# AFNO on Trainium2: the second chunk's remainder rows copied block by block, and the scratch read of the other chunks' rows issued one slot behind their writes

## The chip, the cores and the metric

The kernel runs on one core of one Trainium2 chip. The metric is device time in microseconds (us) of one execution. The kernel before takes 1431.06 us, the median of three timed runs (1430.18, 1431.06 and 1435.22 us). One further execution was profiled.

The core's engines are named as the profile names them: PE (matmul; PEld is its weight load), ACT (ScalarE), DVE (VectorE), POOL (GpSimd) and SP, which here only issues DMAs. Each engine works through its own list of instructions in order and waits on semaphores of the others.

## The reference

Two blocks in a row: an AFNO block (a 2-D FFT over 4096 positions, per-block complex MLP on the frequencies, shrinkage, inverse FFT) and a SwiGLU feed-forward block, both behind an adaptive layer norm. The change lies in the AFNO block. Cut to it:

```python
def _A_ref(x, w1, b1, w2, b2):               # x: 1 x 1 x 4096 x 640, NB = 4 blocks of BS = 160 channels
    Xf = rfft2(x, axes=(1, 2))
    z = Xf.reshape(B, H, Wf, NB, BS)
    zr, zi = z.real, z.imag
    hr = einsum('bhwni,nio->bhwno', zr, w1[0]) - einsum('bhwni,nio->bhwno', zi, w1[1]) + b1[0]
    hi = einsum('bhwni,nio->bhwno', zi, w1[0]) + einsum('bhwni,nio->bhwno', zr, w1[1]) + b1[1]
    hr, hi = relu(hr), relu(hi)
    or_ = einsum(hr, w2[0]) - einsum(hi, w2[1]) + b2[0]
    oi_ = einsum(hi, w2[0]) + einsum(hr, w2[1]) + b2[1]
    # soft shrinkage of both by 0.01, then irfft2
x = x + ga * _A_ref(layernorm(x) * (1 + ca) + sa, ...)
x = x + gb * _B_ref(layernorm(x) * (1 + cb) + sb, ...)      # silu(x @ w_gate) * (x @ w_up) @ w_down
```

## The kernel before

**Chunks and slots.** The frequencies are worked off in 8 chunks (0 to 7) of four blocks each. One pass of the loop at L833 is called a slot here: slot p handles chunk ch = p // 4 and block b = p % 4, for p = 0 to 28. In slot p the PE does the first MLP layer of block p (`stage_l1`, L652, matmuls L667 and L680), the second DFT stage of a block that comes later (`stage_b`, L593, matmul L599), the second MLP layer of block p - 1 (`stage_l2`, L701, matmul L717) and the inverse DFT of block p - 6 (`stage_i`, L753, matmul L763).

**The remainder rows.** A block has 160 channels, but a matmul takes 128 rows. So `stage_b` runs five times per chunk: t = 0 to 3 for the first 128 channels of each block, and t = 4 for the last 32 channels of all four blocks together. The fifth result must be regrouped: the first layer needs, for each block, a tile slice `rz[:, b]` of 128 partitions in which the 32 channels stand four times (real and imaginary part, each as a high and a low half in reduced float32). The kernel before has two ways to do that:

- **Chunk 0: block by block.** `evac_rh` (L633, ACT, two copies of 32x256 at L639) takes the high halves of one block straight from PSUM into `rz`, `evac_rl` (L642, DVE, two operations of 32x256 at L649) the low halves. The result of `stage_b(0, 4)` stays in its PSUM bank (tag `b1`) until the fourth block is copied. The list `rows` at L853 says which blocks are copied in which slot.
- **Chunks 1 to 7: through scratch memory.** `evac_b` (L602) takes the whole result with one ACT copy (L607) and one DVE operation (L608) of 128x512 into `z`; `move_r` (L619) then has SP issue four writes of 128 KB to a DRAM scratch `rzd` (L623) and one read of 512 KB back into `rz` (L625). The read waits for the writes.

**What sets the order.** The order of this part is written out by hand, one list per engine. SP's list around the change, for chunk ch + 1, is: in slot 4 ch (b = 0) the four moves of the chunk before (`move_x`, L736, `xx<-tt`, 320 KB each), in slot 4 ch + 1 the four writes and the read of `move_r`, in slot 4 ch + 3 the loads of the chunk after (`load_g`, L306, 1280 KB, and `load_tb`, L296, 256 KB). For chunk 1 the writes and the read stand in slot 2, and `load_g(2)` behind them. A dictionary `mods` adds in most slots a load of 320 KB of `w_mod` (`mod_load`, L534) at the end of the slot; a load waits for the DVE addition (`mod_add`, L539 and L541) that frees its buffer. SP stops at a read that waits, and all its later DMAs with it. Towards the end of the chunks `load_first_rows` (L828) reads back parts of the result.

The feed-forward block behind that (from L1399 on) is ordered by a planner at build time; the change does not touch it.

```python
        if q[1] < 4 or q[0]:                 # L848: all but the remainder rows of chunk 0
            evac_b(*q)
    ...
    rows = [p + 2] * (p < 2)                 # L853
    ...
    if todo and todo[0][1] == 4:             # L880: the slot of stage_b(ch + 1, 4)
        move_r(todo[0][0])
```

Of the kernel before, what the change touches and what calls it, by code (L numbers as in the profile page):

```python
# [21 lines left out]
NCH = 8  # L22
# [149 lines left out]
def body(tc, x, w1, b1, w2, b2, wg, wu, wd, c, wm, k_fa, k_tb, k_tx, k_bm, k_bx, k_ga, k_ge, k_id, out, dbg=None):  # L172
    nc = tc.nc
# [3 lines left out]
    def f32(ap):  # L177
        return ap.bitcast(F32)
# [21 lines left out]
    with ExitStack() as top:  # L200
# [35 lines left out]
        with ExitStack() as af:  # L236
# [40 lines left out]
            def weights_high(w, h, l, v, sg, eng=None):  # L277
                if eng:
                    eng.tensor_scalar(w[:, :, h], v, sg, None, op0=OP.mult)
                else:  # L280
                    act.activation(w[:, :, h], v, AF.Copy if isinstance(sg, float) else AF.Identity, scale=sg)

            def weights_low(w, h, l, v, sg):
                dve.scalar_tensor_tensor(w[:, :, l], v, sg, f32(w[:, :, h]), op0=OP.mult, op1=OP.subtract)
# [9 lines left out]
            def load_tb(ch):  # L294
                tb = lp.tile([P, 4, 128], F32, tag="tb", bufs=2, name=f"tb{ch}")
                nc.sync.dma_start(tb, k_tb[:, 4 * ch:4 * ch + 4])  # L296
                tbs[ch] = tb


            def load_g(ch, us=None):  # L300
                if ch not in gs:
                    gs[ch] = fx.tile([P, 4, D], F32, tag="gx", bufs=2, name=f"g{ch}")
                f, e = (ch, 1) if ch < 2 else (2, 2) if ch < 4 else (3, 4)
                src = s1[f].rearrange("(u v) (q e j) d -> e u (v q) (j d)", u=4, e=e, q=4)[ch % e]
                if us is None:
                    nc.sync.dma_start(gs[ch].rearrange("p j d -> p (j d)"), src.rearrange("u r d -> r u d"))  # L306
                else:
                    for u in us:
                        nc.sync.dma_start(gs[ch][u:P:4].rearrange("p j d -> p (j d)"), src[u])
# [276 lines left out]
            rzs = {}  # L586
            hss = {}
            rzd = [nc.dram_tensor(f"rzd{i}", (4, 32, NB, 258), F32, kind="Internal").ap() for i in range(2)]

            def width(ch):  # L590
                return 258 if ch == CE else 256

            def stage_b(ch, t, tag=None):  # L593
                g, tb = gs[ch], tbs[ch]
                pb = (ps.tile([P, 2, 256], F32, tag=tag, name=f"pb{ch}_{t}") if tag else
                      bank0(1 if t == 4 else 0, [P, 2, 256], f"pb{ch}_{t}"))
                col = slice(128 * t, 128 * t + 128)
                for j in range(4):
                    mm(pb[:, :, 64 * j:64 * j + 64], g[:, j, col], tb[:, j, :], start=True, stop=True)  # L599
                pbs[ch, t] = pb  # L600

            def evac_b(ch, t):  # L602
                pb = pbs[ch, t]
                z = (lp.tile([P, 2, 2, 258], F32R, tag="z", bufs=4, name=f"z{ch}_{t}") if t < 4 else
                     hp.tile([P, 2, 2, 258], F32R, tag="zr", bufs=1, name=f"z{ch}_{t}"))
                zs[ch, t] = z
                act.activation(z[:, 0, :, 0:256], pb, AF.Identity, scale=ca1[:, t:t + 1])  # L607
                dve.scalar_tensor_tensor(z[:, 1, :, 0:256], pb, ca1[:, t:t + 1],  # L608
                                         f32(z[:, 0, :, 0:256]), op0=OP.mult, op1=OP.subtract)
                if ch == CE:  # L610
                    pool.tensor_copy(z[:, 0, :, 0:257:256], f32(edge[:, 0, t]))
                    pool.tensor_copy(z[:, 1, :, 0:257:256], f32(edge[:, 1, t]))
                    pool.tensor_copy(z[:, :, :, 257], zero[:, 0, 0])


            def new_r(ch):
                rzs[ch] = hp.tile([P, NB, 258], F32R, tag="rz", bufs=2, name=f"rz{ch}")

            def move_r(ch):  # L619
                NN = width(ch)  # L620
                d = rzd[ch % 2]
                for q in range(4):
                    nc.sync.dma_start(d[q, :, :, :NN].rearrange("r b e -> b r e"), f32(zs[ch, 4][:, q // 2, q % 2, :NN]))  # L623
                new_r(ch)
                nc.sync.dma_start(f32(rzs[ch][:, :, :NN]), d[:, :, :, :NN].rearrange("q r b e -> (q r) b e"))  # L625

            def evac_r(ch, b, part=None):
                if part != 1:
# [104 lines left out]
            def move_x(ch, i):  # L733
                q, h = i // 2, i % 2
                xx = p2.tile([P, D], F32, tag="xx", bufs=5, name=f"xx{ch}_{i}")
                nc.sync.dma_start(xx, tts[ch, q][64 * h:64 * h + 64])  # L736
                xxs[ch, i] = xx
# [88 lines left out]
            def load_first_rows(lo, hi, q, e=slice(0, D)):  # L826
                for k in range(2):
                    q.dma_start(cf[k][lo:hi, :, e], s2[lo:hi, 2 * k:2 * k + 2, e])  # L828
# [4 lines left out]
            for p in range(LAST + 1):  # L833
                ch, b = p // 4, p % 4
                on(shrink, p - 6)
                on(stage_l1, p)


                if p < 4:
                    todo = ([(0, 2)], [(0, 3)], [(1, 4), (1, 0)], [(1, 1)])[p]  # L840
                elif b == 0:
                    todo = [(ch, 3)]
                else:
                    todo = [(ch + 1, 4)] * (b == 1) + [(ch + 1, b - 1)]
                todo = [q for q in todo if q[0] < NCH]
                for q in todo:
                    stage_b(*q)
                    if q[1] < 4 or q[0]:  # L848
                        evac_b(*q)
                for f, *a in sums.get(p, ()):  # L850
                    f(*a)

                rows = [p + 2] * (p < 2)  # L853
                for k in rows:
                    on(evac_rh, k)
                if p == 0:
                    weights_high(*prep2[4])
                on(tail_l1, p)
                if p == 0:
                    weights_low(*prep2[2])  # L860
                for k in rows:
                    on(evac_rl, k)
                if p == 3:
                    adds = []
                    stage_l2(0, 2, held=adds)
                    stage_b(1, 2)
                    evac_b(1, 2)
                    on(tail_low, p)
                    for f in adds:
                        f()  # L870
                else:
                    on(tail_low, p)
                    on(stage_l2, p - 1)
                on(stage_i, p - 6)
                if p < LAST:
                    on(shrink_parts, p - 5)
                if b == 0 and ch:
                    for i in range(4):
                        move_x(ch - 1, i)
                if todo and todo[0][1] == 4:  # L880
                    move_r(todo[0][0])
                if p == 0:
                    weights_low(*prep2[4])
                    pool.memset(zero, 0.0)
                    pool.tensor_copy(edge, zero)
                    nc.sync.dma_start(bm.rearrange("p a b -> p (a b)"), k_bm)
                if p == 2 or b == 3 and 2 < ch + 2 < NCH:
                    load_g(ch + 2)
                    load_tb(ch + 2)
                for f, *a in mods.get(p, ()):  # L890
                    f(*a)
                if p == LAST - 4:
                    cf += [rp.tile([P, 2, D], F32, tag=tag, name=f"cf{tag}") for tag in ("rm", "rr")]
                    load_first_rows(rb + 16, rl, nc.sync)
                elif p == LAST - 1:
                    load_first_rows(0, rb - 16, nc.sync)
# [154 lines left out]
        with ExitStack() as ff:  # L1051
# [161 lines left out]
            def chain(at=None):  # L1213
                c = Chain()
                chains.insert(len(chains) if at is None else at, c)
                return c
# [162 lines left out]
            rows = [[chain() for _ in range(4)] for _ in range(NT)]  # L1379
# [1058 lines left out]
            for t in range(NS):  # L2438
                for n in range(NW):
                    if sum_at(n) == t:  # L2440
                        a, b = sum_w(n)
# [81 lines left out]
```

## Time and profile before

| | |
|---|---|
| median of three timed runs | 1431.06 us |
| profiled execution, its own time | 1424.83 us |
| its span (first to last instruction) | 1423.0 us |
| PE / DVE / ACT / POOL busy in the span | 1384.5 / 1025.1 / 722.7 / 620.0 us |
| the AFNO chunks (slots 0 to 28 and the tail) | about 56 to 290 us of the span |
| DMA, mean over the span | 270 GB/s |

The views used below are: the page's overview of the span in 40 slices; the list of waits of one engine in a window (who waited for whom: us in total, times, longest); the timeline of one engine (start, duration, line, tiles, and in brackets the idle time before and what ended it; `x3` means three instructions merged in one row); and the busy time by window, whose columns are the window, its length, busy time and count of PE, PEld, DVE, ACT and POOL, the granted TensorE clock as a share of full speed, the busy share of the 16 DMA engines and GB/s. Names are `out<-in` with buffer numbers left out, so `rz<-rzd` is the read of any chunk.

### The profile page before, as it was taken

What the parts mean: (1) busy time and instruction counts of PE and PEld (TensorE: products, weight loads), DVE (VectorE), ACT (ScalarE), POOL (GpSimd) and SP (SyncE); (2) the same over time, 40 slices, a digit from 0 to 9 for tenths busy, and PEclk for the clock granted to TensorE, in tenths of its full rate; (3) what the DMA queues carried; (4) which work ended last, traced back from release to release, by engine and by line L of the source; (5) the groups of instructions that cost most, each with busy time, mean ns of one, the idle gap of its engine ahead of it and who ended that gap; (6) DMA issues with size and microseconds to landing.
All of it is one profiled execution on the core that took longest, in us unless ns stands there. A gap on an engine that the chain in (4) does not pass through costs nothing. (4 is left out here: it accounts for less than half of the span.)

```text
span 1423.0 us, 23711 instructions
## 1 busy us (share of the span) xinstructions
PE 1384.5 (97%) x8466; PEld 1295.4 (91%) x8466; DVE 1025.1 (72%) x1784; ACT 722.7 (51%) x1465; POOL 620.0 (44%) x696
## 2 busy tenths in 40 slices
PE   6979999999999999999999999999999999999999
PEld 2679899867988888899999999999999999999998
DVE  8947666679898698738786758687668756375654
ACT  7847677536554554526463546445255525252341
POOL 5701211136867575417454625346244525052241
PEclk9989999999999999999999999999999999999999
DMA  9966777776798998798968998787999767966534
GB/s 375 322 225 199 222 236 213 214 213 227 260 331 299 331 329 291 262 387 304 327 214 309 335 340 281 280 283 228 374 338 301 245 218 251 363 205 206 200 121 148
DMA packets 178023, 384.50 MB, mean 270 GB/s; under 512 B 22417, under 2 KB 88657, under 8 KB 175890
## 3 DMA queue, kind: packets, MB, share of 16 engines
q1 hardware_dynamic: 168498, 366.70, 74.3%
q0 software_dynamic: 7104, 13.67, 3.6%
q10 hardware_dynamic: 2304, 2.62, 0.5%
q8 instruction: 67, 1.10, 0.3%
q14 instruction: 50, 0.41, 0.1%
HBM read 272.96 MB, written 100.47 MB: 262 GB/s over the span
## 5 line engine op out<-in xcount | busy, mean ns | idle before, releaser
L1426 DVE TENSOR_TENSOR wb<-r,wb 128x768 fp32r<-128x768 f32 (+3 forms) x170 | 172.7, 1027 | 15.0 <-ACT wb L1419 14.8
L2034 PE MATMUL pw<-h,wt 128*128 128x384 f32 x412 | 139.4, 338 | 0.7 <-ACT s_y L2053 0.6
L2036 PE MATMUL pw<-h,wt 128*128 128x384 f32 x412 | 138.3, 336 | 0.0
L2035 PE MATMUL pw<-h,wt 128*128 128x384 f32 x412 | 138.1, 335 | 0.0
L2335 PE MATMUL pc<-wq,L 128*128 128x320 f32 x846 | 132.7, 309 | 0.5 <-DMA wq<-wqd 0.5
L1419 ACT ACTIVATE wb<-r 128x768 fp32r<-128x768 f32 (+3 forms) x168 | 104.5, 638 | 56.4 <-PE pw L2047 41.4
L2094 POOL TENSOR_TENSOR sg<-s_x,sg 128x384 f32<-128x384 f32 x24 | 30.0, 1248 | 233.2 <-DVE s_x L2060 233.2
L2335 PEld LDWEIGHTS pc<-wq,L 128*128 128x128 f32 x846 | 126.3, 188 | 0.7 <-issue 0.7
L2114 DVE TENSOR_TENSOR L<-sg,L 128x384 fp32r<-128x384 f32 x144 | 100.9, 725 | 27.9 <-ACT L L2110 27.4
L767 POOL DMA_DIRECT2D s<-co x56 | 33.4, 601 | 180.8 <-ACT co L765 180.1
L2053 ACT ACTIVATE s_x<-pw 128x384 f32<-128x384 f32 x52 | 25.6, 492 | 166.4 <-PE pw L2036 165.1
L2034 PE MATMUL pw<-h,wb 128*128 128x384 f32 x312 | 105.0, 336 | 0.0
L2035 PE MATMUL pw<-h,wb 128*128 128x384 f32 x312 | 104.4, 335 | 0.0
L2036 PE MATMUL pw<-h,wb 128*128 128x384 f32 x312 | 104.4, 335 | 0.0
L2105 POOL TENSOR_TENSOR sg<-sg,sg 128x384 f32<-128x384 f32 x72 | 92.0, 1278 | 23.1 <-DVE L L2114 19.7
L1957 PE MATMUL pg<-ht,wb 128*128 128x512 f32 x260 | 101.8, 392 | 0.0
L2335 PE MATMUL pe<-wq,L 128*128 128x320 f32 x648 | 101.7, 309 | 0.0
L1958 PE MATMUL pg<-ht,wb 128*128 128x512 f32 x260 | 101.3, 390 | 0.0
L1959 PE MATMUL pg<-ht,wb 128*128 128x512 f32 x260 | 101.2, 389 | 0.0
L2251 PE MATMUL pd<-wq,a 128*128 128x320 f32 x632 | 96.8, 310 | 0.0
L2335 PEld LDWEIGHTS pe<-wq,L 128*128 128x128 f32 x648 | 96.6, 188 | 0.0
L2251 PEld LDWEIGHTS pd<-wq,a 128*128 128x128 f32 x632 | 93.5, 188 | 0.5
(307 smaller groups left out, 3773.1 us busy)
## 6 DMA issues: line engine op xcount, KB each, us to landing
wq<-wqd SPq DMA_DIRECT2D x83, 640.0 KB
wt<-td SPq DMA_DIRECT2D x103, 512.0 KB
hs<-ho SPq DMA_DIRECT2D x52, 512.0 KB
h<-hs SPq DMA_DIRECT2D x32, 768.0 KB
td<-wt SPq DMA_DIRECT2D x25, 512.0 KB
r<-in_B_w_gate_dram SPq DMA_DIRECT2D x24, 384.0 KB
r<-in_B_w_up_dram SPq DMA_DIRECT2D x24, 384.0 KB
xx<-tt SPq DMA_DIRECT2D x28, 320.0 KB
```

The costliest lines, as they stand in the source:

```text
L1419: def high(ks, e=slice(0, c), copy=lambda o, i: act.activation(o, i, AF.Copy)):
L1426: dve.tensor_tensor(wbs[t, n][:, 1, ks, e], raw[t, n][:, ks, e], f32(wbs[t, n][:, 0, ks, e]), op=OP.subtract)
L1957: mm(b, wh, hh, start=(kk == 0), stop=False)
L1958: mm(b, wh, hl, start=False, stop=False)
L1959: mm(b, wl, hh, start=False, stop=(kk == 4))
L2034: mm(b, w(0, kp), a[:, kp, 0], start=start and kp == 0, stop=False, skip_group_check=not start)
L2035: mm(b, w(0, kp), a[:, kp, 1], start=False, stop=False, skip_group_check=not start)
L2036: mm(b, w(1, kp), a[:, kp, 0], start=False, stop=kp == 1, skip_group_check=not start)
L2105: pool.tensor_tensor(o, x, y, op=op)
L2114: dve.tensor_tensor(o[:, 1], raws[j], f32(o[:, 0]), op=OP.subtract)
L2251: mm(b[:, :320], l, m, start=start and i == 0, stop=stop and i == len(s) - 1)
L2335: mm(o[:, :320], ls[q][:, x, k], w[:, q, y], start=start and q == 0 and n == 0, stop=q == 1 and n == 2, skip_group_check=not start)
```

## The change

Three edits. The remainder rows of chunk 1 are copied block by block like those of chunk 0: `evac_b(1, 4)` and the scratch transfer of chunk 1 go, and `rows` now names block 4 in slot 2, blocks 5 and 6 in slot 3 and block 7 in slot 4. The four writes of chunks 2 to 7 stay where they were. Their read becomes a function of its own, `read_r`, which is called in the next slot (b = 2).

```diff
@@ move_r
                 for q in range(4):
                     nc.sync.dma_start(d[q, :, :, :NN].rearrange("r b e -> b r e"), f32(zs[ch, 4][:, q // 2, q % 2, :NN]))
+
+            def read_r(ch):
+                NN = width(ch)
                 new_r(ch)
-                nc.sync.dma_start(f32(rzs[ch][:, :, :NN]), d[:, :, :, :NN].rearrange("q r b e -> (q r) b e"))
+                nc.sync.dma_start(f32(rzs[ch][:, :, :NN]),
+                                  rzd[ch % 2][:, :, :, :NN].rearrange("q r b e -> (q r) b e"))
@@ the loop over slots
                 for q in todo:
                     stage_b(*q)
-                    if q[1] < 4 or q[0]:
+                    if q[1] < 4 or q[0] > 1:
                         evac_b(*q)
...
-                rows = [p + 2] * (p < 2)
+                rows = [p + 2] * (p < 4) + [p + 3] * (2 < p < 5)
...
-                if todo and todo[0][1] == 4:
-                    move_r(todo[0][0])
+                if b == 1 and 0 < ch < NCH - 1:
+                    move_r(ch + 1)
+                if b == 2 and 0 < ch < NCH - 1:
+                    read_r(ch + 1)
```

Lines behind L625 move by 4 to 6 in the changed kernel: L639 becomes L643, L649 L653, L667 L671, L719 L723, L736 L740; the read is L628 there.

The order of the instructions on each engine shows the edits at three places. In the rows, `z1_4` is chunk 1, t = 4; `wm0_2` is the third of five loads for one vector of `w_mod`; a number at the end is a buffer.

SP, from slot 2 to slot 7. Before:

```order
L625 DMA rz1_900<-rzd1 128x4x256
L306 DMA g2_902<-s12 128x1x2560
L296 DMA tb2_904<-in_k_tb_dram 128x512
L534 DMA wm0_0_983<-in_w_mod_dram 128x640
L736 DMA xx0_0_1054<-tt0_0_797 128x1x640
```

```order
L623 DMA rzd0<-z2_4_1107 4x32x256 x4
L625 DMA rz2_1146<-rzd0 128x4x256
L534 DMA wm0_2_1149<-in_w_mod_dram 128x640
L534 DMA wm0_3_1235<-in_w_mod_dram 128x640
L306 DMA g3_1320<-s12 128x1x2560
```

And now, the same stretch in one piece (the rows ahead of it end with the small loads `tx`, `bx` and `bm`, as before):

```order
L296 DMA tb2_900<-in_k_tb_dram 128x512
L534 DMA wm0_0_987<-in_w_mod_dram 128x640
L740 DMA xx0_0_1062<-tt0_0_797 128x1x640
L740 DMA xx0_1_1064<-tt0_0_797 128x1x640
L740 DMA xx0_2_1066<-tt0_1_808 128x1x640
L740 DMA xx0_3_1068<-tt0_1_808 128x1x640
L534 DMA wm0_1_638<-in_w_mod_dram 128x640
L623 DMA rzd0<-z2_4_1115 4x32x256 x4
L534 DMA wm0_2_1155<-in_w_mod_dram 128x640
L628 DMA rz2_1240<-rzd0 128x4x256
L534 DMA wm0_3_1243<-in_w_mod_dram 128x640
L306 DMA g3_1328<-s12 128x1x2560
```

The five DMAs of chunk 1 are gone, so `load_g(2)` follows the small loads at once. For chunk 2 (and in the same way for 3 to 7) one `mod_load`, the one of the slot of the writes, has moved ahead of the read; nothing else stands between the writes and the read.

ACT, slots 2 and 3, before and now:

```order
L607 ACTIVATE z1_4_863<-pb1_4_858,ca1_68 128x2x256
L607 ACTIVATE z1_0_871<-pb1_0_866,ca1_68 128x2x256
L692 ACTIVATE r2_0_2_855<-u1_0_2_854 64x256
L670 ACTIVATE h32_0_3_0_915<-pl0_3_0_906,b1m_81 128x256
L671 ACTIVATE h0_3_0_916<-pl0_3_0_906,b1m_81 128x256
L670 ACTIVATE h32_0_3_1_929<-pl0_3_1_920,b1m_81 128x256
L671 ACTIVATE h0_3_1_930<-pl0_3_1_920,b1m_81 128x256
L684 ACTIVATE u0_0_3_940<-pl0_3_2_934 64x256
L607 ACTIVATE z1_1_950<-pb1_1_945,ca1_68 128x2x256
L692 ACTIVATE r2_0_3_942<-u1_0_3_941 64x256
L607 ACTIVATE z1_2_977<-pb1_2_972,ca1_68 128x2x256
```

```order
L607 ACTIVATE z1_0_868<-pb1_0_863,ca1_68 128x2x256
L643 ACTIVATE rz1_871<-pb1_4_858,ca1_68 32x256 x2
L696 ACTIVATE r2_0_2_855<-u1_0_2_854 64x256
L674 ACTIVATE h32_0_3_0_911<-pl0_3_0_902,b1m_81 128x256
L675 ACTIVATE h0_3_0_912<-pl0_3_0_902,b1m_81 128x256
L674 ACTIVATE h32_0_3_1_925<-pl0_3_1_916,b1m_81 128x256
L675 ACTIVATE h0_3_1_926<-pl0_3_1_916,b1m_81 128x256
L688 ACTIVATE u0_0_3_936<-pl0_3_2_930 64x256
L607 ACTIVATE z1_1_946<-pb1_1_941,ca1_68 128x2x256
L643 ACTIVATE rz1_871<-pb1_4_858,ca1_68 32x256 x4
L696 ACTIVATE r2_0_3_938<-u1_0_3_937 64x256
L607 ACTIVATE z1_2_981<-pb1_2_976,ca1_68 128x2x256
```

One copy of 128x512 went, two small ones came in slot 2 and four in slot 3, ahead of the activation `r2` of that slot.

DVE, slot 4, now (before, the same rows without `rz1`):

```order
L676 TENSOR_TENSOR h1_0_1_1013<-h32_1_0_1_1012,h1_0_1_1013 128x256
L689 SCALAR_TENSOR_TENSOR u1_1_0_1024<-pl1_0_2_1017,b1r_82,u0_1_0_1023 64x256
L608 SCALAR_TENSOR_TENSOR z1_3_1033<-pb1_3_1028,ca1_68,z1_3_1033 128x2x256
L653 SCALAR_TENSOR_TENSOR rz1_871<-pb1_4_858,ca1_68,rz1_871 32x256 x2
L701 SCALAR_TENSOR_TENSOR r2_1_0_1025<-u1_1_0_1024,r2_1_0_1025 64x256
L723 TENSOR_TENSOR tt0_0_797<-pc0_3_0_1042,b2t_111 128x2x160
L723 TENSOR_TENSOR tt0_1_808<-pc0_3_1_1052,b2t_111 128x2x160
```

The copies of block 7 stand ahead of the additions `tt0`, for which SP's moves `xx0` wait.

## The prediction

> **What bounds the kernel now.** The page's overview first: the PE is busy in almost every slice, and its clock is full in almost all. A change off the PE's path is worth nothing here; one that closes a gap of the PE is worth the gap.
>
> ```profile
> PE   6979999999999999999999999999999999999999
> PEclk9989999999999999999999999999999999999999
> ```
>
> The third digits of both rows (71 to 107 us) show the only dent behind the start. The list of the PE's waits from 60 to 480 us names it: two waits for the read `rz<-rzd`, one of 9.6 us; the next in the list is 1.9 us.
>
> ```profile
> PE pl L667 <- DMA rz<-rzd: 12.3, 2, 9.6
> PE py L1672 <- DVE chl L1662: 1.9, 1, 1.9
> ```
>
> The PE's timeline places both waits, and gives an undisturbed slot (slot 8) to compare with:
>
> ```profile
> 81.74 0.59 PE L667 MATMUL pl<-z,w1a 128*128 128x256 f32 x3
> 82.17 0.52 PE L667 MATMUL pl<-z,w1b 128*128 128x256 f32 x3
> 92.30 0.80 PE L667 MATMUL pl<-rz,w1c 128*128 128x256 f32 x2 [9.62 <-DMA rz<-rzd]
> ...
> 97.16 0.68 PE L717 MATMUL pc<-w2a,h 128*128 128x320 f32 x3
> ...
> 99.57 0.52 PE L667 MATMUL pl<-z,w1a 128*128 128x256 f32 x3
> ...
> 119.39 0.62 PE L667 MATMUL pl<-z,w1a 128*128 128x256 f32 x3
> ...
> 120.20 0.40 PE L667 MATMUL pl<-rz,w1c 128*128 128x256 f32 x2
> ...
> 121.99 1.05 PE L599 MATMUL pb<-tb,g 128*128 128x128 f32 x8
> 122.79 0.69 PE L717 MATMUL pc<-w2a,h 128*128 128x320 f32 x3
> ...
> 268.05 0.79 PE L667 MATMUL pl<-rz,w1c 128*128 128x256 f32 x2 [2.72 <-DMA rz<-rzd]
> ```
>
> The wait of 9.62 us is in slot 4, the first that needs chunk 1's `rz`; the 2.72 us are in slot 28, chunk 7. Slot 5 begins at 99.57, slot 8 at 119.39: a slot is some 6.6 us. SP's timeline says why chunk 1's read is late:
>
> ```profile
> 64.77 10.73 SPq L353 DMA_DIRECT2D s<-xa  x10
> ...
> 79.27 0.45 SPq L886 DMA_DIRECT2D bm<-in_k_bm_dram  x1
> 79.81 2.31 SPq L623 DMA_DIRECT2D rzd<-z  x4
> 88.34 0.58 SPq L625 DMA_DIRECT2D rz<-rzd  x1
> 89.15 0.59 SPq L306 DMA_DIRECT2D g<-s  x1
> ...
> 104.91 2.58 SPq L623 DMA_DIRECT2D rzd<-z  x4
> 114.80 0.57 SPq L625 DMA_DIRECT2D rz<-rzd  x1
> 115.46 1.07 SPq L534 DMA_DIRECT2D wm<-in_w_mod_dram  x2
> ...
> 263.96 0.59 SPq L625 DMA_DIRECT2D rz<-rzd  x1
> ```
>
> SP is busy issuing stores until 79.81; the read can go only at 88.34, 8.5 us after the writes, and the PE starts 3.96 us later.
>
> **Part 1, chunk 1 without scratch.** The wait goes, and its after-effect. From its first L667 to its first L717 slot 4 takes 97.16 - 81.74 = 15.42 us, slot 8 with the same matmuls 122.79 - 119.39 = 3.40 us. The difference is **12.02 us**: 9.62 of waiting, and 2.40 because the PE comes back slow. The windows show that:
>
> ```profile
> 86.00:87.00 1.00, 0.00 (x0) 0.00 (x0) 0.00 (x0) 0.00 (x0) 0.00 (x0) 0.92 0.27 85
> ...
> 96.00:97.00 1.00, 1.00 (x7) 1.00 (x7) 0.68 (x2) 0.29 (x1) 0.00 (x0) 0.50 0.48 183
> 97.00:98.00 1.00, 1.00 (x9) 1.00 (x9) 0.00 (x0) 0.56 (x1) 0.00 (x0) 0.96 0.12 34
> ```
>
> The granted clock begins to fall at 86 to 87 us (0.92) and is still 0.50 at 96 to 97, long after the wait's end at 92.30.
>
> What is late next in slot 4 and 5? `load_g(2)` (1280 KB), issued at 89.15, is through the DMA engines by about 97 (their share falls from 0.48 to 0.12), some 8 us. Now it follows `bm`, at about 79.8: landed near 88. The PE needs it in slot 5, after 81.74 + 3.40 + 2.41 (slot 4 without the stall; its L717 group from 97.16 to 99.57) + 2.6 of first layer (119.39 to 121.99) = 90.2. That holds, with 2 us to spare.
>
> **Part 2, the copies.** Eight ACT copies and eight DVE operations come, one of each of 128x512 goes:
>
> ```profile
> L608 DVE SCALAR_TENSOR_TENSOR z<-pb,ca,z 128x512 fp32r<-128x512 f32 x12 | 9.0, 748 | 5.6 <-ACT z L607 5.3
> L607 ACT ACTIVATE z<-pb,ca 128x512 fp32r<-128x512 f32 x12 | 8.3, 690 | 4.8 <-PE pb L599 4.6
> ...
> L649 DVE SCALAR_TENSOR_TENSOR rz<-pb,ca,rz 32x256 fp32r<-32x256 f32 x8 | 3.9, 483 | 0.5 <-ACT rz L639 0.2
> L639 ACT ACTIVATE rz<-pb,ca 32x256 fp32r<-32x256 f32 x8 | 3.7, 468 | 0.6 <-DVE rz L649 0.3 <-PE pb L599 0.2
> ```
>
> ACT: 8 x 0.468 - 0.69 = 3.1 us more; DVE: 8 x 0.483 - 0.75 = 3.1 us more, over three slots. Slot 2 gets one pair for the 128x512 that goes (+0.2 us each): nothing. Slot 3 gets two. There the engines wait:
>
> ```profile
> 78.78 0.69 ACT L607 ACTIVATE z<-pb,ca 128x512 fp32r<-128x512 f32 x1 [0.18 <-PE pb L599]
> ...
> 82.02 0.69 ACT L607 ACTIVATE z<-pb,ca 128x512 fp32r<-128x512 f32 x1 [2.25 <-PE pb L599]
> ```
>
> ```profile
> 82.74 0.75 DVE L608 SCALAR_TENSOR_TENSOR z<-pb,ca,z 128x512 fp32r<-128x512 f32 x1 [2.49 <-ACT z L607]
> ```
>
> ACT's four copies run from 79.47 to 81.34, inside its idle 2.25 us; DVE's four, if they start only then, end at 83.27, 0.53 us after 82.74. The PE's next user of that PSUM bank (slot 4's L599) comes 2.60 us after the slot's begin (121.99 - 119.39), at 84.34, and the bank is then free at 83.49 + 0.53 = 84.02: no wait, by 0.3 us. Without that cover the PE would lose the overhang, bounds 0 and 0.5 us; I take 0, since the cover is there.
>
> Slot 4 gets one pair, ahead of the additions `tt0`. SP's moves `xx0` wait for these, so chunk 2's chain (moves, writes, read) starts 0.97 to 0.97 + 0.53 = 1.50 us later as seen from the PE. How much slack has its read? It needs 3.96 us from issue to PE in chunk 1 and 268.05 - 263.96 = 4.09 in chunk 7; from 114.80 that is 118.8 to 118.9, and up to 0.9 later (320 KB at some 375 GB/s, a window further down), because POOL's two stores of 160 KB each run just then, on engines that had been idle:
>
> ```profile
> 114.00:115.00 1.00, 1.00 (x10) 1.00 (x10) 0.00 (x0) 0.97 (x2) 1.00 (x2) 1.00 0.00 1
> 115.00:116.00 1.00, 1.00 (x11) 1.00 (x10) 0.75 (x2) 1.00 (x4) 0.25 (x1) 1.00 0.81 164
> ```
>
> The PE needs it at 120.20: slack 0.4 to 1.4 us. So slot 8 gets a **new wait** of 0 to 1.1 us. I take **0.6**, the middle, and keep both ends.
>
> **Part 3, the read one slot behind.** SP reaches it after one more `mod_load`, but what it waits for is the landing of the writes, 8.5 us (79.81 to 88.34) and 9.9 us (104.91 to 114.80) after their issue, longer than one slot (6.6 us). So the read of chunk 2 still goes when its writes have landed. The `mod_load` moved ahead waits for a DVE addition of its slot, which ends at 107.4:
>
> ```profile
> 106.83 0.54 DVE L539 TENSOR_SCALAR acc<-wm,sc 128x640 f32<-128x640 f32 x1
> ```
>
> That is 7 us before the landing. Its 320 KB then go while the writes leave three quarters of the DMA engines idle (0.27 at 86 to 87 us), or in the idle window 114 to 115: cost 0, bounds 0 and 0.9 us per read (320 KB at 375 GB/s). It gains nothing either: the loads it speeds up are waited for by no PE row. Chunk 7's wait of 2.72 us stays, since its writes and their landing do not move.
>
> **Sum.** -12.0 + 0.6 = **-11.4 us**. Behind the chunks every list shifts as a whole; I find no start that depends on the clock instead of on the PE's progress. Span 1423.0 - 11.4 = 1411.6; the profiled execution 1424.83 - 11.4 = 1413.4; it lies 6.2 us under the median of the timed runs, 1431.06, from which I predict **1419.7 us**.
>
> **Rivals.**
>
> *The slow clock at slot 28 does not come back* (15%). There a wait of 2.72 us was enough for the slow clock:
>
> ```profile
> 267.00:268.00 1.00, 0.00 (x0) 0.00 (x0) 0.00 (x0) 0.00 (x0) 0.00 (x0) 0.88 1.03 375
> 268.00:269.00 1.00, 0.95 (x4) 0.95 (x5) 0.02 (x1) 0.12 (x1) 0.00 (x0) 0.50 1.16 374
> ...
> 271.00:272.00 1.00, 1.00 (x10) 1.00 (x10) 0.49 (x2) 0.81 (x3) 0.00 (x0) 0.92 0.99 415
> ```
>
> [...] Half speed from 268.05 to about 271.2 costs 1.6 us: 1418.1. [...]
>
> *The moved load delays the reads* (12%). It stands ahead of each read in the same queue. At 0.9 us per read, chunk 7 loses 0.9, chunk 2 another 0.9, the four between up to 0.9 each, less a slack that I know only to be positive (no wait of theirs is in the list): 1.8 to 5.4 us, about 1423. Against it: the idle DMA window before the read. [...]
>
> *The gain is absorbed later* (8%): the next stage is bound by something that does not start earlier.
>
> ```profile
> 320.00:360.00 40.00, 37.36 (x175) 30.14 (x174) 38.29 (x50) 25.47 (x43) 29.17 (x29) 1.00 0.68 222
> ```
>
> For it: DVE is busy 38.29 of 40 us there and the PE idles 2.6. Against it: DVE's list starts earlier too, and the DMA engines are 0.68 busy. If half were lost: about 1425.
>
> *Slower* (3%). The read stands behind a `mod_load` that waits for DVE. If DVE's addition ended after the writes' landing instead of 7 us before, each of six reads would be late by the excess x. 6x minus the slacks (at most 1.4 each for five) outweighs 11.4 from x = 1.9 to 3.1 us on. At x = 6.6, one slot: up to 40 us lost, about 1455.
>
> *The wait only changes its name* (2%): `load_g(2)` lands after 90.1 for all that, for instance behind the last stores; each us late is one us lost, 1431 at 11.4.
>
> **How the numbers follow.** My forecast holds with 60%. The range reaches from the clock rival without the new wait (1417.5, and 2 for the scatter of the runs, 1430.18 to 1435.22) to the absorbed half: **1415.5 to 1425**. A difference of 0.5% (7.2 us, to 1423.9) is about what a measurement of this kernel can tell. Faster 86% (forecast, clock, three quarters of the moved load), same 10%, slower 4%.
>
> **What would show it.** Right: no wait for DMA at slot 4's `rz` matmul, clock 1.00 through 80 to 100 us, slot 5 starting near 87.6 in the timeline, the wait list with `rz<-rzd` near 3.3 us in two waits (slot 8 and slot 28), SP's `g<-s` at about 80. Wrong in part 2: a PE wait for DVE at L599 of slot 4, or over 1.1 us at slot 8. Wrong in part 3: `rz<-rzd` over 4.1 us from issue to PE, or more than two such waits. Wrong at all: a span above 1415.

## The result and the profile after

| | before | changed |
|---|---|---|
| median, lowest, highest of 10 runs each | 1430.71 (1427.50 to 1435.22) us | 1421.45 (1418.80 to 1428.39) us |
| ratio of the times, 95% interval | | 0.9941 [0.9922, 0.9960] |
| profiled execution / its span | 1424.83 / 1423.0 us | 1421.29 / 1419.5 us |

The changed kernel is faster, by 9.3 us of the medians; the interval of the ratio is a gain of 5.7 to 11.2 us. Forecast were 11.4 us, 0.2 us beyond that interval; in a second group of runs (`e3_changed_again`, below) the gain of the medians is 9.6 us and its interval, 6.9 to 13.9 us, includes the forecast. The dent in the page's overview is gone, PE and granted clock:

```profile
PE   6899999999999999999999999999999999999999
PEclk9999999999999999999999999999999999999999
```

The windows of slots 4 and 5 say the same: in the changed kernel the PE is busy in all of the 20 us, at a granted clock (third number from the right) of 1.00. The kernel before (the second row) had 10.38 us of PE work there and a mean clock of 0.74.

```profile
80.00:100.00 20.00, 20.00 (x161) 20.00 (x160) 16.08 (x34) 15.55 (x33) 0.00 (x0) 1.00 0.58 174
```

```profile
80.00:100.00 20.00, 10.38 (x65) 10.18 (x64) 5.42 (x12) 3.74 (x8) 0.00 (x0) 0.74 0.47 161
```

The next two views are the two longest entries in the list of the changed kernel's PE waits from 40 to 480 us, and the places of the waits that matter in its timeline. (L783 was L779; it computes the inverse DFT's edge columns and needs a `g` that SP loads.)

```profile
PE pl L671 <- DMA rz<-rzd: 2.8, 2, 2.5
PE px L783 <- DMA g<-s: 2.4, 1, 2.4
```

```profile
65.69 1.16 PE L599 MATMUL pb<-tb,g 128*128 128x128 f32 x8 [1.12 <-DVE z L608]
68.86 0.38 PE L721 MATMUL pc<-w2c,r 128*128 128x320 f32 x1 [1.08 <-DVE r L701]
...
85.87 0.59 PE L671 MATMUL pl<-z,w1a 128*128 128x256 f32 x3
...
91.78 0.52 PE L671 MATMUL pl<-z,w1a 128*128 128x256 f32 x3
...
111.60 0.62 PE L671 MATMUL pl<-z,w1a 128*128 128x256 f32 x3
112.86 0.50 PE L671 MATMUL pl<-rz,w1c 128*128 128x256 f32 x2 [0.29 <-DMA rz<-rzd]
...
146.73 1.25 PE L783 MATMUL px<-tx,g 128*128 128x2 f32 x10 [2.45 <-DMA g<-s]
...
263.91 0.50 PE L671 MATMUL pl<-rz,w1c 128*128 128x256 f32 x2 [2.51 <-DMA rz<-rzd]
```

Slot 4 has no wait and takes 91.78 - 85.87 = 5.91 us, where it took 99.57 - 81.74 = 17.83: the 11.9 us are gone. But it begins at 85.87 instead of 81.74, and slot 12 has a wait for `g<-s` of 2.45 us, where the profile of before has one of 0.69 us for ACT. The table sets slots against each other, each from the first L667 (L671) of a slot to that of the next named one, in us; "again" are two further profiles of the same two kernels (experiments `e10_before_again` and `e3_changed_again`).

| profile | slot 4 begins | 4 to 5 | 8 to 9 | 12 to 13 | 13 to 28 | 28 to 29 | 29 to the end | span |
|---|---|---|---|---|---|---|---|---|
| before | 81.74 | 17.83 | 6.61 | 8.64 | 107.84 | 12.10 | 1146.59 | 1423.05 |
| before, again | 83.31 | 16.04 | 6.60 | 11.92 | 107.84 | 14.08 | 1149.29 | 1430.79 |
| changed | 85.87 | 5.91 | 7.16 | 11.95 | 107.84 | 12.09 | 1146.97 | 1419.49 |
| changed, again | 82.31 | 5.90 | 7.08 | 8.55 | 107.84 | 12.32 | 1147.01 | 1412.71 |

The changed kernel's first profile lies 7.9 us above the forecast span of 1411.6. Its start, 4.13 us later, and slot 12, 3.31 us longer, are 7.4 of these; the second profile, with hardly any of either, has 1412.7. Both things occur in the unchanged kernel too (second row), so neither needs the change. But a later start should then show in the times of both kernels alike. Why it doesn't is the question of the experiments.

Part of the late start is a slow clock of its own. Slot 1 begins 1.35 us later than in the kernel before (61.84 against 60.49), slot 2 3.13 us (71.71 against 68.58) and slot 3 4.14 us (79.33 against 75.19). The first two rows above are waits in slot 1, of 1.12 and 1.08 us, and behind them, from 71 to 74 us, the granted clock reads 0.50, 0.50 and 0.54, where the kernel before has 1.00: slot 2 takes 7.62 us, against 6.61 there and 6.65 in the second profile of the changed kernel.

This is SP's list, in which `load_g(2)` now goes at 80.07 and chunk 2's read follows its writes by 10.3 us (9.9 us before):

```profile
80.07 0.57 SPq L306 DMA_DIRECT2D g<-s  x1
...
93.41 3.68 SPq L740 DMA_DIRECT2D xx<-tt  x4
...
98.41 2.61 SPq L623 DMA_DIRECT2D rzd<-z  x4
101.12 1.01 SPq L534 DMA_DIRECT2D wm<-in_w_mod_dram  x1
108.75 0.58 SPq L628 DMA_DIRECT2D rz<-rzd  x1
```

### The profile page after: what moved, and what is told of

The parts are those of the page before. It is cut to its first block, busy times and chain, and to the rows that moved or that the text cites. A ratio compares the mean times of both kernels' runs of the same rounds, so it can differ in the third digit from the quotient of the medians.

```text
span 1419.5 us, 23715 instructions
## 1 busy us (share of the span) xinstructions
PE 1386.6 (98%) x8466; PEld 1296.2 (91%) x8466; DVE 1036.5 (73%) x1791; ACT 725.9 (51%) x1472; POOL 619.0 (44%) x696
## 5 line engine op out<-in xcount | busy, mean ns | idle before, releaser
L1432 DVE TENSOR_TENSOR wb<-r,wb 128x768 fp32r<-128x768 f32 (+3 forms) x170 | 169.9, 1010 | 11.9 <-ACT wb L1425 11.7
```

Of the source, the lines that this page charges most:

```text
L1432: dve.tensor_tensor(wbs[t, n][:, 1, ks, e], raw[t, n][:, ks, e], f32(wbs[t, n][:, 0, ks, e]), op=OP.subtract)
```

## The experiments

The kernels of one group ran side by side, with the kernel before beside them (17 or 23 runs of it in a group).

| kernel | median us (runs) | before beside it | ratio, 95% interval |
|---|---|---|---|
| `e1_copies_only` | 1423.05 (6) | 1432.28 | 0.9935 [0.9916, 0.9954] |
| `e2_late_read_only` | 1430.23 (12) | 1432.28 | 0.9986 [0.9973, 0.9998] |
| `e3_changed_again` | 1422.67 (6) | 1432.28 | 0.9928 [0.9903, 0.9952] |
| `e4_early_g` | 1419.70 (6) | 1432.28 | 0.9906 [0.9882, 0.9930] |
| `e5_wait_kept_busy` | 1435.18 (12) | 1432.23 | 1.0027 [1.0012, 1.0042] |
| `e6_wide_scratch` | 1413.57 (6) | 1432.23 | 0.9879 [0.9856, 0.9902] |
| `e7_wide_scratch_before` | 1418.46 (6) | 1432.23 | 0.9906 [0.9884, 0.9927] |
| `e8_copies_twice` | 1429.81 (12) | 1432.23 | 0.9978 [0.9961, 0.9996] |
| `e9_wait_kept_busy_less` | 1430.98 (12) | 1431.47 | 1.0001 [0.9983, 1.0018] |
| `e10_before_again` | 1431.88 (12) | 1431.47 | 1.0009 [0.9995, 1.0024] |
| `e11_wide_early_g` | 1413.47 (6) | 1431.47 | 0.9893 [0.9873, 0.9913] |
| `e12_delay_before_wait` | 1432.09 (12) | 1433.33 | 0.9995 [0.9978, 1.0013] |

### The parts alone

**The copies alone**: the changed kernel with the read back in the slot of its writes.

```diff
                 if b == 1 and 0 < ch < NCH - 1:
                     move_r(ch + 1)
-                if b == 2 and 0 < ch < NCH - 1:
                     read_r(ch + 1)
```

> Chunk 1 copied block by block as in the change; the read of chunks 2 to 7 back in the slot of its writes, ahead of the mod_load. Theory A (all of the gain is the copies; the order of the read does nothing): the time of the changed kernel, ratio to before 0.992 to 0.996, slot 4 without a wait. Theory B (the mod_load that moved ahead shares DMA engines with the writes, so these land later; this made the wait at the edge columns of slot 12 and its slow clock, 3.3 us): 2 to 3 us faster than the change, ratio 0.990 to 0.993, and no wait for g<-s at L783 (edges).

It has the whole gain, as far as the intervals can tell: 0.9935, and the changed kernel 0.9928 in the same group. Slot 4 takes 5.90 us. Slot 12 waits for `g<-s` in its trace as well, though no load stands at another place in SP's list:

```profile
143.57 2.07 PE L783 MATMUL px<-tx,g 128*128 128x2 f32 x10 [2.54 <-DMA g<-s]
```

So the moved `mod_load` isn't needed for slot 12's wait.

**The late read alone**: the kernel before, with `read_r` one slot behind `move_r` for chunks 2 to 7.

```diff
-                if todo and todo[0][1] == 4:
-                    move_r(todo[0][0])
+                if p == 2:
+                    move_r(1)
+                    read_r(1)
+                if b == 1 and 0 < ch < NCH - 1:
+                    move_r(ch + 1)
+                if b == 2 and 0 < ch < NCH - 1:
+                    read_r(ch + 1)
```

> Chunk 1 through scratch as before; only the read of chunks 2 to 7 one slot later, behind one mod_load. Theory A: no difference to before, ratio 0.999 to 1.001, slot 4 waits 9 to 10 us. Theory B: 2 to 3 us slower, ratio 1.001 to 1.003, chunk 3's writes land over 17 us after the start of slot 9 (before 15.6, change 18.0).

The ratio is 0.9986, a gain of at most 3.9 us and at least 0.3; the value lies just under the lower of the two expected ranges (0.999 to 1.001). From slot 13 to slot 28 its trace takes 107.86 us, `e1_copies_only` 107.85, the kernels of the table above 107.84: for chunks 4 to 6, whose rows are first used there, the place of the read is worth nothing. That `e1` and `e3` have the same time (1423.05 and 1422.67) speaks for this too, and the rival of the prediction in which the moved load delays the reads falls. Slot 28, which waits for chunk 7's read, lies outside this stretch. It took 12.1 to 14.5 us in the five traces with the late read and the old writes, and 12.1 to 18.0 us in the six without the late read (18.02 in `e1_copies_only`, where the wait is of 4.2 us and the page's overview has 8 tenths of granted clock from 249 to 285 us, 9 in all other slices). So whether 0 or some 2 us of the gain belong to the late read isn't settled.

**The changed kernel again**, unedited:

> The changed kernel once more, for what differs from profile to profile. If the 4.1 us that slots 0 to 3 lost in the first profile (no instruction of theirs was changed ahead of slot 2) are chance, slot 4 starts nearer to 82 us than to 86 and the span is 2 to 4 us shorter. If the wait at L783 of 2.4 us comes from the change, it is there again; if it is chance, it is gone or under 1 us.

It is the last row of the table above: with an early start and no long wait in slot 12, the span is 1412.7 us.

**The load of `g` ahead of the moves**: in the changed kernel, `load_g(ch + 2)` for chunks 3 to 7 goes from the end of slot 4 ch + 3 to slot 4 ch, ahead of `move_x`.

```diff
+                if b == 0 and 0 < ch < NCH - 2:
+                    load_g(ch + 2)
                 if b == 0 and ch:
                     for i in range(4):
                         move_x(ch - 1, i)
...
+                if p == 2:
+                    load_g(2)
                 if p == 2 or b == 3 and 2 < ch + 2 < NCH:
-                    load_g(ch + 2)
                     load_tb(ch + 2)
```

> The change, and load_g for the chunk after issued at b = 0 ahead of the moves instead of at b = 3 behind the read. The wait at L783 for g<-s goes in any case. If that wait and its slow clock (3.3 us) are a part of the changed kernel's time, 2 to 3 us faster than the change, ratio 0.990 to 0.993. Rival: 1280 KB (3.5 us of the DMA engines) ahead of moves, writes and read make all of these up to 3.5 us later, waits for rz<-rzd appear at several slots, and it is slower than the change by 2 us or more.

Slot 12's wait is gone (12 to 13 is 7.70 us instead of 11.95), so that load was what it waited for. 1419.70 us is 3 us under the changed kernel in the same group, but the intervals overlap, and slot 28 took 14.46 us in its trace, 2.4 more than in the changed kernel's: part of the gain was not kept there.

### The wait, its slow clock, and the cover of the copies

**Slot 4's wait kept busy**: the kernel before, with products of a tile of ones by itself (`idle`, L332) on the PE ahead of slot 4's first layer, 60 of them, then 35 (the diff with 35 in place of 60).

```diff
                 on(shrink, p - 6)
+                if p == 4:
+                    idle(60)
                 on(stage_l1, p)
```

> The kernel before, with 60 matmuls of 128x128 on a constant tile put ahead of slot 4's first layer, about 8 us of work inside the wait of 9.62 us; their result is not used. If the 2.4 us behind that wait are the slow clock, the clock stays 1.00, a wait of 1 to 3 us for rz<-rzd is left, and slots 3 to 5 take 24.4 - 2.2 = 22.2 us or a little more; the time is 1 to 2.5 us shorter than before. If the slow matmuls behind the wait have another cause (the read's data, the DMA traffic then), slots 3 to 5 still take 24.4 us.

> As e5, with 35 instead of 60 of the constant products. In e5 each went out as two matmuls of 0.11 us, so that 60 filled 13.6 us, more than the wait; 35 fill 7.9 us. If the slow clock makes the 2.4 us behind the wait, a wait of 1 to 2.5 us for rz<-rzd is left, the clock there stays 1.00, and slots 3 to 5 take 22 to 22.5 us instead of 24.4; 1.5 to 2.5 us shorter than before. If not, 24.4 us and no gain.

The 60 products took 13.56 us, 0.11 us for each of 120 matmuls (a product of float32 is two of them here), which is more than was meant. They outlast the wait, and the kernel is 3 us slower instead of 1 to 2.5 us faster. What the trace tells of the clock holds for all that. These are slots 4 and 5 behind the filling, with 60 products and with 35:

```profile
98.05 0.59 PE L667 MATMUL pl<-z,w1a 128*128 128x256 f32 x3
...
103.85 0.51 PE L667 MATMUL pl<-z,w1a 128*128 128x256 f32 x3
```

```profile
91.54 0.60 PE L667 MATMUL pl<-z,w1a 128*128 128x256 f32 x3
...
97.35 0.52 PE L667 MATMUL pl<-z,w1a 128*128 128x256 f32 x3
```

Slot 4 takes 5.80 and 5.81 us, with the same data from the same read, and the granted clock reads 1.00 from 84 to 104 us with 60 products and from 84 to 97 us with 35. In the kernel before it takes 99.57 - 92.30 = 7.27 us from the wait's end on alone, when a part of the first layer was done already. So the clock after the wait is a cost of its own, and the PE kept busy didn't pay it in these two traces. The 35 products gained nothing in the median all the same (1.0001, where 1.5 to 2.5 us were expected). Why is open: in its one trace the stretch from slot 3 to slot 5 took 20.17 us, against 24.38 and 22.58 in the two profiles of the kernel before. That in other executions the filling outlasts a shorter wait is a guess.

**The copies twice**: the changed kernel, with each copy of blocks 5 to 7 of the remainder rows done twice.

```diff
                 for k in rows:
-                    on(evac_rh, k)
+                    for _ in range(2 if k > 4 else 1):
+                        on(evac_rh, k)
...
                 for k in rows:
-                    on(evac_rl, k)
+                    for _ in range(2 if k > 4 else 1):
+                        on(evac_rl, k)
```

> The change, with the copies of blocks 5, 6 and 7 made twice (same values): six ACT and six DVE operations more, 2.8 and 2.9 us. If the copies are hidden as long as they fit into the idle time of slots 3 and 4 (2.25 us of ACT, 2.49 of DVE), the doubled ones no longer fit: slot 3's eight end 2 us later, the PE waits 1 to 2.5 us for DVE z at L599 of slot 4, and chunk 2's read is late by another 1 us or more, so that slot 8's wait grows from 0.3 to 1 to 2 us: 2 to 4 us slower than the change. If DVE and ACT have more room than I think, no difference.

In the changed kernel DVE's four copies of slot 3 end at 87.54 and the `z` operation behind them at 87.57 + 0.75 = 88.32. Slot 4's L599 comes 2.57 us after 85.87, at 88.44 (DVE first, then the PE):

```profile
85.57 1.97 DVE L653 SCALAR_TENSOR_TENSOR rz<-pb,ca,rz 32x256 fp32r<-32x256 f32 x4 [1.18 <-ACT rz L643]
87.57 0.75 DVE L608 SCALAR_TENSOR_TENSOR z<-pb,ca,z 128x512 fp32r<-128x512 f32 x1
```

```profile
88.44 1.10 PE L599 MATMUL pb<-tb,g 128*128 128x128 f32 x8
```

With the copies doubled the same place reads, on DVE and on the PE:

```profile
88.31 4.04 DVE L653 SCALAR_TENSOR_TENSOR rz<-pb,ca,rz 32x256 fp32r<-32x256 f32 x8 [3.18 <-ACT rz L643]
92.37 0.75 DVE L608 SCALAR_TENSOR_TENSOR z<-pb,ca,z 128x512 fp32r<-128x512 f32 x1
```

```profile
93.18 2.08 PE L599 MATMUL pb<-tb,g 128*128 128x128 f32 x8 [3.85 <-DVE z L608]
```

The PE waits 3.85 us, and behind the wait the clock is halved (0.50 in each window of 1 us from 92 to 98 us): slot 4 takes 12.17 us instead of 5.91, 6.3 more, of which 2.4 are the clock. The ratio went from 0.9928 or 0.9941 to 0.9978, 5 to 7 us, where 2 to 4 us were expected, without the clock and with a wait of 1 to 2.5. The wait is longer than that because DVE starts only when ACT's copies are done, so that the longer runs of both add up: ACT's took 3.90 instead of 1.91 us, DVE's 4.04 instead of 1.97, together 4.06 more. Of these all but 0.2 us became a wait. So in the changed kernel the copies are hidden, with 0.1 to 0.2 us to spare.

### Who sets the end of slot 4's wait

**The kernel before again**, unedited:

> The kernel before, unchanged, for a second profile. If waits that come and go with no edit (the start, slots 0 to 3; g<-s or nothing at slot 12; 2.5 to 4.8 us at slot 28) separate its profiled execution of 1424.8 us from its median of 1431, this profile shows two or three of them, 3 to 7 us in all, while slots 3 to 5 again take 24.4 us within 0.5. If the wait of slot 4 itself is what varies, slots 3 to 5 differ by over 2 us.

The longer waits of slots 12 and 28 are there as expected (table above), but the stretch from slot 3 to slot 5 took 22.58 us, 1.8 less than in the first profile: more than the 0.5 us allowed for a wait that stays, and less than the 2 us expected of one that varies. Slot 4 began later there, and its wait was shorter.

**A delay ahead of the wait**: the kernel before with 12 products of `idle` in slot 2. They were meant as 2.7 us. In the trace they hold the PE from 72.37 to 76.51, 4.14 us, or 0.17 us for each of 24 matmuls, where those of `e5_wait_kept_busy` took 0.11.

```diff
                 on(shrink, p - 6)
+                if p == 2:
+                    idle(12)
                 on(stage_l1, p)
```

> The kernel before, with 12 constant products (24 matmuls, 2.7 us, result not used) ahead of slot 2's first layer: a start-up that is late on purpose. Theory C (in the kernel before, the end of slot 4's wait is set by SP's list of stores, which does not depend on the PE, so a late PE only waits less; the changed kernel pays such a delay in full): slot 4 starts 2.7 us later than it would, its wait is 9.6 - 2.7 - (the other start-up delay of 0 to 5) us, slot 5 starts at 99.3 to 101.5 us as in the other profiles of the unchanged kernel, and the time is that of the kernel before, ratio 0.9990 to 1.0010. Theory D (the delay goes through, as the sum of the prediction took it): slot 5 starts at 102 us or later and the time is 2 to 3 us longer, ratio 1.0015 to 1.002.

These are slot 4, its wait and slot 5 in the second profile of the kernel before, and then SP's writes and read of chunk 1 there:

```profile
83.31 0.59 PE L667 MATMUL pl<-z,w1a 128*128 128x256 f32 x3
...
92.39 0.80 PE L667 MATMUL pl<-rz,w1c 128*128 128x256 f32 x2 [8.13 <-DMA rz<-rzd]
...
99.35 0.52 PE L667 MATMUL pl<-z,w1a 128*128 128x256 f32 x3
```

```profile
80.10 2.32 SPq L623 DMA_DIRECT2D rzd<-z  x4
88.56 0.58 SPq L625 DMA_DIRECT2D rz<-rzd  x1
```

The same with the delay, PE and SP:

```profile
72.37 4.38 PE L332 MATMUL pz<-ones 128*128 128x128 f32 x24
...
89.75 0.59 PE L667 MATMUL pl<-z,w1a 128*128 128x256 f32 x3
...
93.95 0.80 PE L667 MATMUL pl<-rz,w1c 128*128 128x256 f32 x2 [3.25 <-DMA rz<-rzd]
...
101.58 0.51 PE L667 MATMUL pl<-z,w1a 128*128 128x256 f32 x3
```

```profile
81.53 2.33 SPq L623 DMA_DIRECT2D rzd<-z  x4
90.10 0.58 SPq L625 DMA_DIRECT2D rz<-rzd  x1
```

And slot 4 in the trace of the late read alone, which has the same wait:

```profile
86.73 0.59 PE L671 MATMUL pl<-z,w1a 128*128 128x256 f32 x3
...
93.96 0.80 PE L671 MATMUL pl<-rz,w1c 128*128 128x256 f32 x2 [6.28 <-DMA rz<-rzd]
...
101.44 0.52 PE L671 MATMUL pl<-z,w1a 128*128 128x256 f32 x3
```

Against the first profile of the kernel before, slot 4 begins 1.57, 4.99 and 8.01 us later in these three, and slot 5 0.22 earlier, 1.87 and 2.01 later. (The order is: second profile of the kernel before, late read alone, delay.) What slot 5 follows is the read, which was issued 0.22, 1.83 (at 90.17) and 1.76 us later than the 88.34 of the first profile. The wait swallows the rest: it shrinks from 9.62 to 8.13, 6.28 and 3.25 us. The delay didn't move SP: its ten stores `s<-xa` begin at 66.60 us there, ahead of the delay, and at 64.77 in the first profile, so SP was 1.8 us late already. In the trace slot 5 begins at 101.58, between the two expectations (101.5 at most, 102 at least); the median decides, in which the delay costs nothing (0.9995, interval of 1.0013 at most, which is 1.9 us). So in the kernel before the PE's delays ahead of slot 4 are free up to the length of the wait. In the changed kernel slot 5 follows slot 4 by 5.90 and 5.91 us whether this begins at 82.31 or at 85.87, so that a late start goes through to slot 5; no run put a delay into it.

### The scratch writes themselves

In the prediction's window of 86 to 87 us the writes ran with a DMA share of 0.27, and in the kernel before the windows from 82 to 87 us read 0.26 to 0.28. A write goes into the scratch as 4 blocks of 32 rows. An estimate from the share is that some 4 of the 16 engines are at work (0.27 x 16 = 4.3). That the 4 blocks are the reason was an assumption of the author's; the runs below have another layout.

**Wide writes**: the scratch laid out so that a write goes row by row (128 rows), and the read split into four of 32 partitions; in the changed kernel, then in the kernel before (same lines, L625), then in the changed kernel with the early load of `e4_early_g`.

```diff
-  rzd = [nc.dram_tensor(f"rzd{i}", (4, 32, NB, 258), ...
+  rzd = [nc.dram_tensor(f"rzd{i}", (4, NB, 32, 258), ...
...
-  nc.sync.dma_start(d[q, :, :, :NN].rearrange("r b e -> b r e"), ...
+  nc.sync.dma_start(d[q, :, :, :NN].rearrange("b r e -> (b r) e"), ...
...
-  nc.sync.dma_start(f32(rzs[ch][:, :, :NN]), rzd[ch % 2][:, :, :, :NN].rearrange("q r b e -> (q r) b e"))
+  for q in range(4):
+      nc.sync.dma_start(f32(rzs[ch][32 * q:32 * q + 32, :, :NN]),
+                        rzd[ch % 2][q, :, :, :NN].rearrange("b r e -> r b e"))
```

> The change, with the scratch laid out block by block, so that each of the four writes goes from 128 partitions to 128 rows in order, and the read split into four of 32 partitions. If the writes of chunks 2 to 7 are slow because they use a quarter of the DMA engines, they now land 4 to 6 us earlier; the waits for rz<-rzd (2.5 to 2.8 us in the change, slots 8 and 28) and for g<-s at L783 (0.6 to 2.5 us) go, with their slow clocks, and the time is 4 to 7 us shorter than the change, ratio to before 0.987 to 0.991. If the writes' landing is a fixed delay, or SP's three more issues per chunk (1.7 us) eat it up, nothing is gained: 0.993.

> The kernel before with the same scratch layout and four reads; chunk 1 still goes through scratch. SP's late start (79.8 us) stays, the 8.5 us from the writes to the read should become 3 to 5. Slot 4's wait falls from 9.6 to 4 to 6 us and slots 3 to 5 take 18 to 21 us instead of 24.4. If SP's late start alone set the wait, it stays over 8 us. Either way block copies keep an advantage: the time lies between the kernel before and e6.

> e6 with load_g at b = 0 ahead of the moves, as in e4. e6's profile has no wait left in slots 4 to 28 for DMA, so no gain: ratio to before 0.986 to 0.990, like e6. If the early load of 1280 KB delays moves and writes, waits for rz<-rzd come back and it is 1 to 3 us slower than e6.

The first view shows SP's writes and reads of chunk 2 in the changed kernel with wide writes, the second those of chunk 1 in the kernel before with them, the third slot 4's wait there:

```profile
97.61 2.44 SPq L623 DMA_DIRECT2D rzd<-z  x4
...
103.15 2.93 SPq L629 DMA_DIRECT2D rz<-rzd  x4
```

```profile
80.14 2.02 SPq L623 DMA_DIRECT2D rzd<-z  x4
83.59 1.75 SPq L626 DMA_DIRECT2D rz<-rzd  x4
```

```profile
87.68 0.47 PE L669 MATMUL pl<-rz,w1c 128*128 128x256 f32 x2 [2.98 <-DMA rz<-rzd]
```

From writes to read it is 5.5 us instead of 10.3 in chunk 2, 3.5 instead of 8.5 in chunk 1. That is the writes' doing, since the read, whose form changed too, comes behind it. In the changed kernel with wide writes the DMA share is 1.20 and 1.03 in the two windows ahead of chunk 2's read (101 to 103 us, 274 and 233 GB/s, with a load of 320 KB issued at 100.14 among it). With the old writes, ahead of the same read, it is 0.27 in both windows from 105 to 107 us, at 84 and 83 GB/s. In the changed kernel with wide writes no wait for `rz` or `g` from a DMA is left in slots 4 to 28: slot 12 and slot 28 take 7.71 and 7.70 us. At 1413.57 us it is 1.2% under the kernel before; the early load adds nothing to it (1413.47).

Wide writes alone, without the change, gain about as much as the change or more (0.9906 [0.9884, 0.9927]; the changed kernel has 0.9941 [0.9922, 0.9960] and 0.9928 [0.9903, 0.9952] in other groups). Slot 4's wait is down to 2.98 us, less than the 4 to 6 that were expected, and the waits of slots 12 and 28 are gone as well. Where the writes are wide, the change is worth only 1418.46 - 1413.57 = 4.9 us of the medians, about half of what it is worth without them, though the intervals of the two ratios overlap.

## Why the prediction was right in direction and some 2 us too large

- **Part 1** was right to 0.1 us for the profile from which it was read: slot 4 to slot 5 fell from 17.83 to between 5.89 and 5.91 us in each version with the copies and no doubling. The slow clock as a part of it is shown by the two kernels with the filled wait (slot 4 in 5.80 and 5.81 us at a clock of 1.00). `load_g(2)` was in time for slot 5.
- **Part 2** was right. The copies lay where the forecast put them, the end of DVE's last operation 0.12 us ahead of slot 4's L599 (0.3 forecast), and `e8_copies_twice` agrees with that little room. SP's moves start 1.63 us after slot 5 begins instead of 0.34, so 1.3 us later (0.97 to 1.50 forecast). With its new wait slot 8 got longer by 0.55 and 0.47 us in the two profiles of the changed kernel, by 0.35 in `e1_copies_only` and not at all in `e4_early_g`; the forecast took 0.6, from 0 to 1.1.
- **Part 3** was right as far as it can be told: 107.84 us from slot 13 to slot 28 with and without it, and two waits for `rz<-rzd`, 4.11 and 4.05 us from the read's issue to the PE.
- **The sum failed in one sentence**: "Behind the chunks every list shifts as a whole; I find no start that depends on the clock instead of on the PE's progress." The start in question lies ahead, not behind. SP's list of stores and small loads, which set the read of chunk 1, moved by at most 1.8 us while the PE's slot 4 moved by 8.0; so slot 4's wait ended at a time of its own, and made good most of what the PE had lost before. The one profile of before had the earliest start of all that were taken, 81.74 us, and therefore the longest wait. Taking the 9.62 us of it off the median of the runs as well was too much. How much too much is near the noise. An estimate of the term from all traces: slot 5 begins at 100.1 us on the mean of the three kernels that keep the wait as it was (99.57, 99.35, 101.44), and at 89.9 on the mean of six that have the copies (91.78, 88.75, 88.21, 90.03, 90.97, 89.72). That is 10.2 us instead of 12.0, and with 0.3 for slot 8, the mean of the four of these with the old writes, 9.9. The runs say 9.3 and 9.6, with intervals of 5.7 to 11.2 and 6.9 to 13.9. Traces of different executions differ elsewhere by as much as these 2 us, so the estimate is no proof.
- **The profiled execution** (1413.4 forecast, 1421.29 measured) was off by the start and by slot 12's wait, 7.4 us together. By the prediction's own sign, a span above 1415 us, this profile (1419.5) spoke against it and the second (1412.7) did not. The prediction didn't ask which waits of a single profile come and go. Slot 12 took 8.6 and 11.9 us in the two profiles of the kernel before, slot 28 12.1 and 14.1, and the part from slot 29 to the end 1146.6 and 1149.3. Together these three differ by 8.0 us, and the two spans by 7.7. So one execution of it can take 1424.83 us when ten others lay between 1427.50 and 1435.22.
- **The rivals.** The slow clock of slot 28 came back: 12.09 us after 12.10, with a wait of 2.51 us and a granted clock of 0.53, 0.50 and 0.50 from 265 to 268 us. That such a wait can pass is true all the same: one of 2.98 us did, in another kernel (last section). The gain was not absorbed later, since slot 29 to the end took 1146.97 and 1147.01 us, after 1146.59 and 1149.29. The moved load fell with `e1_copies_only` and the 107.84 us.
- **Two slips that changed nothing.** Up to 79.81 us SP issues stores and then small loads, not stores alone. And the three chances that the prediction adds up for "faster" make 84% (60, 15 and 9), not 86%.

What stays open: what makes the first slots begin 0.5 to 5 us later from one execution to the next (waits of about 1 us for DVE and a slow clock behind them are a part of it, as shown above; no run tried to remove them), what makes the waits of slots 12 and 28 long or short, and whether the late read is worth anything.

## What to carry to other kernels

Slot 4's wait, whose end SP's own list set, swallowed most of the delays ahead of it: where slot 4 began 8.01 us later, slot 5 began 2.01 later. So the length of such a wait in one profile isn't what its removal is worth: look how far its beginning moves between profiles while its end stands still. Before a transfer is taken off the path, look at the share of the DMA engines that it runs with; here the 0.27 was worth about as much as the whole change (0.9906 for the wide writes alone, 0.9941 and 0.9928 for the change), and it sat in the quoted windows. The copies hidden by an idle gap cost the PE no wait while they ended 0.12 us ahead of its need; past that, in `e8_copies_twice`, they cost a wait of 3.85 us and 2.4 us of slow clock behind it.

## What the runs showed of the hardware that I had not expected

The slow clock did not go by the length of the wait alone. In the kernel before, slot 28's 2.72 us were followed by a clock of 0.50 (268 to 271 us). In the kernel before with wide writes, slot 4's 2.98 us passed at full clock (the windows from 84 to 92 us, clock third from the right):

```profile
84.00:88.00 4.00, 1.02 (x9) 0.84 (x9) 2.06 (x4) 0.69 (x1) 0.00 (x0) 1.00 0.78 200
88.00:92.00 4.00, 4.00 (x34) 4.00 (x33) 1.97 (x4) 3.05 (x7) 0.00 (x0) 1.00 0.94 376
```

In slot 12 of the late read alone, a wait of only 1.09 us is followed by a clock of 0.55:

```profile
155.05 1.25 PE L783 MATMUL px<-tx,g 128*128 128x2 f32 x10 [1.09 <-DMA g<-s]
```

```profile
155.00:157.00 2.00, 1.95 (x16) 1.98 (x17) 1.16 (x4) 0.08 (x1) 0.16 (x1) 1.00 0.07 26
157.00:159.00 2.00, 2.00 (x10) 2.00 (x10) 0.65 (x2) 0.00 (x0) 0.42 (x2) 0.55 0.00 0
```

There the first matmuls behind the wait are of two columns only (`128x2`, ten in 1.25 us); whether the fall of the clock has to do with that, no run shows. And writes of the same 512 KB of chunk 1 took 8.5 us to their read, at a DMA share of 0.27, as 4 blocks of 32 rows, and 3.5 us as 128 rows.
